# k's transposes in one of the MLP's PSUM banks in two slots, ScalarE's copies a tile later, and k's copies ahead of the division in a third

## The chip, the cores and the metric

The kernel runs on one core of one Trainium2 chip. The time is device microseconds of that core, the median over runs of the whole program. Below, "us" is a microsecond, TensorE is the matrix engine (PE in the profile, its weight loads PEld), VectorE is DVE, ScalarE is ACT, GpSimd is POOL and SyncE is SP.

## The reference

A causal attention with a decay on the scores, and behind it a two-layer MLP over all tokens:

```
q, k, v: (8, 8, 576, 64)   f: (8, 8, 576)   w_in: (512, 2048)   w_out: (2048, 512)
cum    = cumsum(log(clip(f, 1e-4, 1)))
scores = q @ k.T / sqrt(64) + cum[i] - cum[j],  -1e9 above the diagonal
attn   = exp(scores - max) / (sum + 1e-9)
x      = (attn @ v), heads side by side          # (4608, 512)
h      = x @ w_in;  g = h - tanh(h);  out = g @ w_out
```

## The kernel before, in words

**Slots.** The 64 heads are 32 pairs; four pairs make one batch element. The main loop (lines 608 to 629) has a slot p for each pair and one more. `att_items(p)` (line 547) writes out by hand the attention work of a slot, in the order in which every engine gets it, and between these items the loop puts steps of the MLP (`TAKE` says how many). Each engine works its own queue in that order; semaphores are added for what is read and written. So the order on an engine never changes at run time: a late instruction holds up all that stand behind it on its engine.

**A slot's attention.** A pair's scores come in seven tiles, ti = 0 to 6. `scores` (line 306) computes one tile with TensorE into one of two PSUM banks (pool `ps_sc`), and ScalarE takes the exponential of it into SBUF (line 335, tile `e`, or `el` for the small tile 3); from batch element 1 on GpSimd then zeroes what lies above the diagonal (line 345). Tile n + 2 takes the bank of tile n, so its matmuls wait for the exponential of tile n. `values` (line 350) does 30 small matmuls of the pair before, at ti = 2 from slot 5 on, and VectorE divides by the row sums: `rs` (lines 364 and 365) and `xn` (line 366). `turn` (line 369) then transposes `xn` into the MLP's input `XR` with two DMAs of SyncE (lines 380 and 382).

**q's and k's transposes.** For batch elements 0 to 2, `trans` (line 254) brings q and k of a pair into head-dimension-first form (`QT`, `KT`): six TensorE transposes into one PSUM bank (line 264, tile `t`), then two copies out of it, one for the even and one for the odd tokens. They write into the same tile at interleaved places, so the second copy waits for the first. From batch element 3 on DMAs do this, and no PSUM is used.

- Slots 0 to 3: the bank comes from the MLP's pool `ps_m` (three banks).
- Slots 4 to 6: the bank is the single one of the pool `ps_tr`, and VectorE does both copies ("VV", line 277). The transposes of q stand at ti = 0, those of k at ti = 2 in slot 4 and ti = 3 in slots 5 and 6, for the pair of the next slot. In slot 6 the k of slot 7 is made this way.
- Slots 7 and 8 (line 569): each makes two pairs of batch element 2, q at ti = 0, k at ti = 2, q at ti = 4, k at ti = 6, all in the one bank of `ps_tr`. Of each, VectorE does the first copy and ScalarE the second ("VA", lines 277 and 275). Both are emitted right behind the transposes.

**The MLP.** `mlp1` (line 398) is one 128-wide piece of h: four 512-column matmuls into a bank, tanh on ScalarE (line 413), and h - tanh(h) on VectorE (line 417, tile `gq`). For the first 512 tokens the second layer is `mlp2_plain` (line 436): 16 steps of four matmuls (line 442), four steps to an output tile of 128 tokens, which ScalarE copies out of its bank (line 446, tile `ost`) and a DMA of SyncE writes out. Slot 6 holds the last `mlp1` steps of these tokens and the first two steps of `mlp2_plain` fall to slots 6 and 7; slots 7 and 8 hold `mlp2_plain` alone, slot 9 its end and the first `mlp1` of the next 512 tokens. `bank` (line 389) hands out the banks; up to slot 8 these are the three of `ps_m`, from slot 9 on (`widen(1)`, line 613) also that of `ps_tr`.

**Other work there.** In slots 7 and 8 VectorE also forms differences of w_out's blocks (`weights`, line 243, at ti = 1, 3 and 5), GpSimd starts the loads of batch element 3's q and k (line 96), and SyncE transposes that q (line 101).

Of the kernel before, what the change touches and what calls it, by code (L numbers as in the profile page):

```python
# [8 lines left out]
FP32 = mybir.dt.float32  # L9
FP16 = mybir.dt.float16  # L10
AF = mybir.ActivationFunctionType
ALU = mybir.AluOpType
# [9 lines left out]
def kernel(  # L22
# [10 lines left out]
    nc = tc.nc  # L33
    P = 128

    B, H, S, D = q.shape
# [4 lines left out]
    NPAIR = H // 2  # L41
    NJ = 5
# [5 lines left out]
    UW = 512  # L48
# [14 lines left out]
    PSUM = bass.MemoryType.PSUM  # L63
    ps_sc = ctx.enter_context(tc.tile_pool(name="ps_sc", bufs=2, space=PSUM))
    ps_av = ctx.enter_context(tc.tile_pool(name="ps_av", bufs=1, space=PSUM))
    ps_tr = ctx.enter_context(tc.tile_pool(name="ps_tr", bufs=1, space=PSUM))
    ps_m = ctx.enter_context(tc.tile_pool(name="ps_m", bufs=3, space=PSUM))

    win = wpl.tile([P, NCH, DFF], FP16)
    wout = wpl.tile([P, NFT, DM], FP16)  # L70
# [10 lines left out]
    qn, kn = ([t[0:S // NT6, :].rearrange("p (h n d) -> p h n d", h=H, n=NT6) for t in raw] for raw in (qraw, kraw))  # L81
# [170 lines left out]
    E, XN, GQ, SQ, M2 = {}, {}, {}, {}, {}  # L252

    def trans(b, c, src, dst, early, copies, split=False):
        pn, g3 = S // NT6, NT6 // 2
        if early:
            t32 = ps_m.tile([P, UW], FP32, tag="m", name="t32")
            t16 = t32.bitcast(FP16)[:, 0:2 * S // 2].rearrange("p (a g n) -> p a g n", a=2, g=g3)
        else:
            t32 = ps_tr.tile([P, UW], FP32, tag="tr", name="t32")  # L260
            t16 = t32.bitcast(FP16)[:, 0:2 * S // 2].rearrange("p (a g n) -> p a g n", a=2, g=g3)
        for a in range(2):
            for g in range(g3):
                nc.tensor.transpose(out=t16[:, a, g, :],  # L264
                                    in_=src[b % 2][:, 2 * c + a, 2 * g:2 * g + 2, :],
                                    identity=id16[0:pn, 0:pn])
        parts = [(a, e) for a in range(2) for e in range(2)] if split else [(slice(0, 2), e) for e in range(2)]

        def copy(a, e, eng):
            if split:  # L270
                a = slice(a, a + 1)
            to = dst[b % 2][0:D, 2 * c:2 * c + 2, e:S:2].rearrange("d a (p g) -> d a p g", g=g3)[:, a]
            of = t16[e * D:(e + 1) * D, :, :, :].rearrange("d a g p -> d a p g")[:, a]
            if eng == "A":
                nc.scalar.activation(out=to, in_=of, func=AF.Copy)  # L275
            else:
                nc.vector.tensor_copy(out=to, in_=of)  # L277

        todo = [lambda a=a, e=e, eng=eng: copy(a, e, eng) for (a, e), eng in zip(parts, copies)]
        for fn in todo[:2]:  # L280
            fn()
        return todo[2:]

    def head_tiles(a):
        return [[(a, 0, 0, 512, 0)],
                [(a, 1, P, 448, 0), (a, 0, 512, 64, 448)],
                [(a, 2, 2 * P, 320, 0), (a, 3, 3 * P, 192, 320)]]

    TILES = head_tiles(0) + [[(0, 4, 512, 64, 64), (1, 4, 512, 64, 128)]] + head_tiles(1)
    LAST = 3  # L290
# [56 lines left out]

    AV = {}

    def values(b, c, heads=(0, 1)):  # L350
        if 0 in heads:
            AV[(b, c)] = ps_av.tile([P, 2, 512], FP32, tag="av", name="av")
        av = AV[(b, c)][:, :, 0:NJ * (D + 1)].rearrange("p a (i d) -> p a i d", i=NJ)
        for a in heads:
            for ib in range(NJ):
                for j in range(ib + 1):
                    nc.tensor.matmul(out=av[:, a, ib, :], lhsT=E.pop((b, c, a, j, ib)),  # L357
                                     rhs=vn[b % 2][:, j, 2 * c + a, 0:D + 1],
                                     start=(j == 0), stop=(j == ib))
        if 1 not in heads:  # L360
            return
        xn = XN[(b, c)] = fin.tile([P, NJ, P], FP16, tag="xn", name="xn")
        rs = fin.tile([P, 2, NJ, 1], FP32, tag="rs", name="rs")
        nc.vector.tensor_scalar_add(out=rs, in0=av[:, :, :, D:D + 1], scalar1=1e-9)  # L364
        nc.vector.reciprocal(out=rs, in_=rs)
        nc.vector.tensor_tensor(out=xn.rearrange("p i (a d) -> p a i d", a=2), in0=av[:, :, :, 0:D],  # L366
                                in1=rs.to_broadcast([P, 2, NJ, D]), op=ALU.mult)

    def turn(b, c):
        xn = XN.pop((b, c))  # L370
        r0 = b % 4 * S
        if b == 0:
            x32 = ps_m.tile([P, UW], FP32, tag="m", name="x32")
            xt = x32.bitcast(FP16)[:, 0:S]
            for ib in (NJ - 1, 0, 1, 2, 3):
                w0 = min(ib * P, S - P)
                nc.tensor.transpose(out=xt[:, w0:w0 + P], in_=xn[:, ib, :], identity=id16)
            nc.scalar.activation(out=XR[:, c, r0:r0 + S], in_=xt, func=AF.Copy)  # L378
            return
        nc.sync.dma_start_transpose(out=XR[:, c, r0:r0 + S - D].rearrange("p (n t) -> p n t", t=P),  # L380
                                    in_=xn[:, 0:NJ - 1, :].rearrange("p n d -> p (n d)"))
        nc.sync.dma_start_transpose(out=XR[:, c, r0 + S - D:r0 + S], in_=xn[D:P, NJ - 1, :])

    HP = {}
    RINGS = [[ps_m], [ps_m, ps_m, ps_m, ps_tr], [ps_m, ps_m, ps_m, ps_tr, ps_sc, ps_sc]]
    TAGS = {ps_m: "m", ps_tr: "tr", ps_sc: "sc"}
    turn_of = [0, 0]

    def bank(name):
        ring = RINGS[turn_of[0]]  # L390
        pool = ring[turn_of[1] % len(ring)]
        turn_of[1] += 1
        return pool.tile([P, UW], FP32, tag=TAGS[pool], name=name)

    def widen(n):
        turn_of[:] = [n, 0]

    def mlp1(u, ft, part=None):
        if part != 1:
            HP[(u, ft)] = bank("hps")  # L400
        hps = HP[(u, ft)]
        t0 = u * UW % RING
        parts = [(0, t0, min(UW, RING - t0))]
        if t0 + UW > RING:
            parts.append((RING - t0, 0, t0 + UW - RING))
        for o, t, n in parts:
            for ci in {None: range(NCH), 0: range(NCH - 1), 1: (NCH - 1,)}[part]:
                nc.tensor.matmul(out=hps[:, o:o + n], lhsT=win[:, ci, ft * P:(ft + 1) * P],  # L408
                                 rhs=XR[:, ci, t:t + n], start=(ci == 0), stop=(ci == NCH - 1))
        if part == 0:  # L410
            return
        th = tmp.tile([P, UW], FP32, tag="th", name="th")
        nc.scalar.activation(out=th, in_=hps, func=AF.Tanh, scale=-1.0)  # L413
        half, i, kt = ft // NK, ft % NK // 4, ft % 4
        if half == 0 and kt == 0:
            GQ[(u, i)] = gtp.tile([P, 2, NK // 2, UW], FP16, tag="gq", name="gq")
        nc.vector.tensor_tensor(out=GQ[(u, i)][:, half, kt, :], in0=hps, in1=th, op=ALU.add)  # L417
        if u >= PLAIN:
            if ft in (3, 6, 9, 12):
                sums(u, "S3", ft // 3 - 1)  # L420
# [126 lines left out]
    def att_items(p):  # L547
        def put(fn, *args):
            items.append((lambda: fn(*args), True))

        items = []
# [4 lines left out]
        for ti in range(len(TILES)):  # L556
# [9 lines left out]
            for load in LOADS.get((p, ti), ()):  # L566
                items.append((load, False))
            at_q, at_k = (1, 3) if p == 0 else (0, 1) if early else (0, 2) if p == NPAIR else (0, 3)
            if p in (2 * NPAIR - 1, 2 * NPAIR) and ti % 2 == 0:
                pair = pairs[2 * NPAIR + 2 * (p - 2 * NPAIR + 1) + ti // 4]  # L570
                put(trans, *pair, *((kn, KT) if ti % 4 else (qn, QT)), False, "VA")
# [7 lines left out]
            if p == NPAIR:  # L579
                if ti == 1:  # L580
                    put(turn, *pairs[p - 2])
                    put(values, *before)
                    put(mlp1, 0, 0, 0)
                elif ti == 2:
                    put(mlp1, 0, 1, 0)
                    put(turn, *before)
            elif early and ti in (2, 3) and before:
                put(values, *before, (ti - 2,))
            elif not early and ti == 2 and before:
                put(values, *before)  # L590
            if p < NPAIR:
                if ti == 1 and p > 1:
                    put(turn, *pairs[p - 2])
            elif p > NPAIR and ti == 3:
                put(turn, *before)
        return items

# [8 lines left out]
    with tc.manual_schedule(engines=FIVE):  # L606
        bulk()
        for p in range(len(pairs) + 1):
            b, c = divmod(p, NPAIR)
            items = att_items(p)  # L610
            take = TAKE[p] if p < len(TAKE) else 8 - (p - len(TAKE)) % 2
            if p == 2 * NPAIR + 1:
                widen(1)
            mine = mlp[at:at + take]
            at += take
# [5 lines left out]
            given, n = 0, 0  # L621
# [39 lines left out]
```

## Time and profile before

| what | value |
|---|---|
| median of 3 runs | 347.94 us (347.92 to 347.96) |
| the profiled execution's own time | 347.95 us |
| its span from first to last instruction | 346.2 us |
| TensorE busy | 335.2 us, 97% of the span |
| VectorE busy | 261.7 us, 76% |
| ScalarE busy | 232.6 us, 67% |
| GpSimd busy | 161.3 us, 47% |

The profile comes from one execution. A row of its timeline gives the start from the beginning of the span, the busy time, the engine, the line, the operation with its output and input and the count of like instructions merged into the row; in brackets stands how long the engine was idle before, and what released it. TensorE's matmuls are pipelined and the ends in the records are modelled: two rows may overlap, and the step from one start to the next is the safer measure of what a group costs. A chain of waits is followed back from the last instruction, at each step to what released it.

### The profile page before, as it was taken

How to read it: one execution, taken by the hardware profiler on the slowest of the kernel's cores; microseconds unless marked ns; L12 is line 12 of the kernel's file. 1: busy time of each engine (PE TensorE's matmuls, PEld its weight loads, DVE VectorE, ACT ScalarE, POOL GpSimd, SP SyncE). 2: the span in 40 equal slices, each digit the busy share in tenths (PEclk: the TensorE clock that was granted, in tenths of full speed). 3: DMA queues.
4: the chain of work that ended last, by engine and by line, in shares of the span. 5: the costliest groups of instructions: out<-in, count | busy, mean ns of one | idle time of the engine just before them, and what ended most of it. 6: DMA issues, size and time to landing. Idle time of an engine off the chain costs nothing.

```text
span 346.2 us, 8606 instructions
## 1 busy us (share of the span) xinstructions
PE 335.2 (97%) x3253; PEld 230.6 (67%) x3253; DVE 261.7 (76%) x504; ACT 232.6 (67%) x437; POOL 161.3 (47%) x319
## 2 busy tenths in 40 slices
PE   8988998889999999999999999999999999999995
PEld 7476554555578656865688888755875587487485
DVE  6599787564988788678867886788677766876874
ACT  5687886777897787778767876788548842632640
POOL 8974652676558655765577465742322210000000
PEclk9999999999999999999999999999999999999999
DMA  8999999999999999799979997991131013003003
GB/s 108 147 182 201 193 201 154 107 114 177 132 130 105 177 137 122 94 176 137 117 78 200 130 128 78 186 143 27 49 97 31 17 50 110 0 14 109 0 11 113
DMA packets 144877, 38.80 MB, mean 112 GB/s; under 512 B 128148, under 2 KB 143236, under 8 KB 144836
## 3 DMA queue, kind: packets, MB, share of 16 engines
q0 software_dynamic: 92480, 18.39, 69.7%
q1 hardware_dynamic: 52356, 19.88, 30.5%
q8 instruction: 25, 0.41, 0.5%
q14 instruction: 16, 0.13, 0.1%
HBM read 36.85 MB, written 9.44 MB: 134 GB/s over the span
## 4 chain that ended last, share of the span: by engine, by line
PE 87%; DVE 6%; ACT 4%; issue 1%; DMA 1%; ACTq 0%
PE hps L408 32%; PE ops L466 28%; PE ps L326 12%; PE av L357 8%; PE ops L442 3%; DVE gq L417 2%; ACT e L335 2%; DVE QT L277 2%; PE t L264 1%; DVE KT L277 1%; PE ps L329 1%; DMA TQ<-in_f_dram 1%; PE ps L297 1%; ACT QT L275 1%; ACT th L413 1%
## 5 line engine op out<-in xcount | busy, mean ns | idle before, releaser
L408 PE MATMUL hps<-XR,win 128*128 128x512 f16 (+1 forms) x640 | 140.9, 357 | 0.9 <-ACT XR L378 0.7
L413 ACT ACTIVATE th<-hps 128x512 f32<-128x512 f32 x144 | 86.9, 603 | 55.4 <-PE hps L408 54.6
L335 ACT ACTIVATE e<-ps 128x512 f16<-128x512 f32 x192 | 110.5, 598 | 14.1 <-PE ps L326 6.0
L417 DVE TENSOR_TENSOR gq<-hps,th 128x512 f16<-128x512 f32 x144 | 98.4, 688 | 26.0 <-ACT th L413 24.6
L345 POOL TENSOR_SCALAR_AFFINE_SELECT e<-e 128x128 f16<-128x128 f16 x168 | 60.4, 361 | 78.0 <-ACT e L335 76.1
L408 PEld LDWEIGHTS <-win 128*128 128x128 f16 x640 | 57.7, 97 | 48.4 <-issue 0.5
L326 PE MATMUL ps<-QT,KT 67*128 67x64 f16 (+5 forms) x384 | 77.9, 276 | 3.1 <-ACT e L335 1.7
L466 PEld LDWEIGHTS <-gq 128*128 128x128 f16 x640 | 60.4, 97 | 11.1
L466 PE MATMUL ops<-wout,gq 128*128 128x256 f16 x512 | 63.2, 272 | 0.0
L326 PEld LDWEIGHTS <-KT 67*128 67x128 f16 (+1 forms) x384 | 36.7, 98 | 25.5 <-DVE KT L277 1.6
L357 PEld LDWEIGHTS <-e 128*128 128x128 f16 x896 | 32.2, 97 | 3.9
L357 PE MATMUL av<-vn,e 128*128 128x65 f16 x896 | 33.6, 193 | 0.0
L119 POOL DMA_DIRECT2D vn<-in_v_dram x32 | 28.0, 878 | 8.7 <-DMA win<-in_moe_w_in_dram 4.1
L466 PE MATMUL ops<-W,sq 128*128 128x256 f16 x256 | 31.2, 272 | 0.0
L366 DVE TENSOR_TENSOR xn<-av,rs 128x640 f16<-128x640 f32 x32 | 26.4, 825 | 1.1
L466 PEld LDWEIGHTS <-sq 128*128 128x128 f16 x256 | 24.2, 98 | 3.4
L96 POOL DMA_DIRECT2D kn<-in_k_dram x25 | 21.2, 848 | 1.5 <-issue 1.3
L345 POOL TENSOR_SCALAR_AFFINE_SELECT el<-el 128x128 f16<-128x128 f16 x28 | 9.4, 334 | 26.9 <-ACT el L335 26.2
L96 POOL DMA_DIRECT2D qn<-in_q_dram x25 | 21.2, 848 | 1.3 <-issue 0.8
L364 DVE TENSOR_SCALAR rs<-av 128x10 f32<-128x10 f32 x32 | 5.2, 162 | 19.0 <-PE av L357 17.9
L277 DVE COPY QT<-t 64x576 f16<-64x576 f16 x18 | 14.5, 803 | 6.2 <-PE t L264 6.1
L277 DVE COPY KT<-t 64x576 f16<-64x576 f16 (+1 forms) x22 | 16.3, 739 | 3.8 <-PE t L264 3.6
(82 smaller groups left out, 307.5 us busy)
## 6 DMA issues: line engine op xcount, KB each, us to landing
out_dram<-ost SPq DMA_DIRECT2D x34, 256.0 KB
vn<-in_v_dram POOLq DMA_DIRECT2D x24, 128.0 KB, 5.6
qn<-in_q_dram POOLq DMA_DIRECT2D x20, 128.0 KB, 4.3
kn<-in_k_dram POOLq DMA_DIRECT2D x20, 128.0 KB, 4.6
win<-in_moe_w_in_dram POOLq DMA_DIRECT2D x2, 1024.0 KB, 14.8
wout<-in_moe_w_out_dram POOLq DMA_DIRECT2D x2, 1024.0 KB, 14.1
XR<-xn SPq DMA_TRANSPOSE x56
vn<-in_v_dram POOLq DMA_DIRECT2D x12, 64.0 KB, 5.2
```

Source lines behind the costliest of these rows:

```text
L96: nc.gpsimd.dma_start(out=dst[b % 2][0:pn, n, :].rearrange("p (h d) -> p h d", h=H), in_=src[b, :, n * P:n * P + pn, :].rearrange("h p d - ...
L119: nc.gpsimd.dma_start(out=vn[b % 2][:, n, h0:h1, 0:D], in_=v[b, h0:h1, n * P:(n + 1) * P, :].rearrange("h p d -> p h d"))
L277: nc.vector.tensor_copy(out=to, in_=of)
L326: nc.tensor.matmul(out=ps[:, col:col + n], lhsT=KT[b % 2][0:rows, h, j * P:(j + 1) * P], rhs=QT[b % 2][0:rows, h, i0:i0 + n], start=not ow ...
L335: nc.scalar.activation(out=e[:, lo:hi], in_=ps[:, lo:hi], func=AF.Exp, scale=qscale)
L345: nc.gpsimd.affine_select(out=view, in_=view, compare_op=ALU.is_ge, fill=0.0, base=0, pattern=pat, channel_multiplier=-1)
L357: nc.tensor.matmul(out=av[:, a, ib, :], lhsT=E.pop((b, c, a, j, ib)), rhs=vn[b % 2][:, j, 2 * c + a, 0:D + 1], start=(j == 0), stop=(j == ib))
L366: nc.vector.tensor_tensor(out=xn.rearrange("p i (a d) -> p a i d", a=2), in0=av[:, :, :, 0:D], in1=rs.to_broadcast([P, 2, NJ, D]), op=ALU. ...
L408: nc.tensor.matmul(out=hps[:, o:o + n], lhsT=win[:, ci, ft * P:(ft + 1) * P], rhs=XR[:, ci, t:t + n], start=(ci == 0), stop=(ci == NCH - 1))
L413: nc.scalar.activation(out=th, in_=hps, func=AF.Tanh, scale=-1.0)
L417: nc.vector.tensor_tensor(out=GQ[(u, i)][:, half, kt, :], in0=hps, in1=th, op=ALU.add)
L466: nc.tensor.matmul(out=ps[:, m, :], lhsT=LHS[lhs](u, kt // 4)[:, kt % 4, m * P:(m + 1) * P], rhs=rhs[:, kt, :], start=(fresh and (apart or ...
```

## The change

- The three banks of `ps_m` get a tag each (`m0`, `m1`, `m2`), and `m_bank` hands them out in turn, as before. `keep()`, called as slot 7 begins, takes the next one out of the turn until slot 9 begins; there k's transposes go in slots 7 and 8, and the MLP has the other two. q's transposes stay in the bank of `ps_tr`.
- In slots 7 and 8 ScalarE's half of each copy is no longer emitted right behind VectorE's half, but put on a list (`LATER`) that is emptied behind the scores of the next tile (`rest`, at ti = 0, 1, 3 and 5; once more at ti = 0 of slot 9).
- In slot 6 the division of the pair before is put on a list (`HELD`), and so is every addition of `mlp1` that comes while the list is not empty; the list is worked off at ti = 3 behind k's copies. So VectorE's order there becomes k's two copies, `rs`, `xn`, `gq`, `gq` in place of `rs`, `xn`, `gq`, the two copies, `gq`.

The order on TensorE, GpSimd and SyncE stays the same, instruction by instruction, and so does the number and shape of all instructions.

```diff
-    ps_m = ctx.enter_context(tc.tile_pool(name="ps_m", bufs=3, space=PSUM))
+    ps_m = ctx.enter_context(tc.tile_pool(name="ps_m", bufs=1, space=PSUM))
+    M_AT, KEPT = [0], []
+
+    def m_bank(name):
+        while M_AT[0] % 3 in KEPT:
+            M_AT[0] += 1
+        M_AT[0] += 1
+        return ps_m.tile([P, 512], FP32, tag=f"m{(M_AT[0] - 1) % 3}", name=name)
+
+    def keep():
+        while M_AT[0] % 3 in KEPT:
+            M_AT[0] += 1
+        KEPT.append(M_AT[0] % 3)
...
         if early:
-            t32 = ps_m.tile([P, UW], FP32, tag="m", name="t32")
+            t32 = m_bank("t32")
+        elif KEPT and src is kn:
+            t32 = ps_m.tile([P, UW], FP32, tag=f"m{KEPT[0]}", name="t32")
         else:
             t32 = ps_tr.tile([P, UW], FP32, tag="tr", name="t32")
...
-        for fn in todo[:2]:
+        now = 1 if copies == "VA" else 2
+        for fn in todo[:now]:
             fn()
-        return todo[2:]
+        if copies == "VA":
+            LATER.extend(todo[now:])
+        return todo[now:]
...
+    LATER = []
+
+    def rest():
+        while LATER:
+            LATER.pop(0)()
...
+    HELD = []
+
+    def release():
+        while HELD:
+            HELD.pop(0)()
+
-    def values(b, c, heads=(0, 1)):
+    def values(b, c, heads=(0, 1), hold=False):
...
-        nc.vector.tensor_scalar_add(out=rs, in0=av[:, :, :, D:D + 1], scalar1=1e-9)
-        nc.vector.reciprocal(out=rs, in_=rs)
-        nc.vector.tensor_tensor(out=xn.rearrange("p i (a d) -> p a i d", a=2), in0=av[:, :, :, 0:D],
-                                in1=rs.to_broadcast([P, 2, NJ, D]), op=ALU.mult)
+        def divide():
...
+        HELD.append(divide)
+        if not hold:
+            release()
...
-        nc.vector.tensor_tensor(out=GQ[(u, i)][:, half, kt, :], in0=hps, in1=th, op=ALU.add)
+        def add_up():
+            nc.vector.tensor_tensor(out=GQ[(u, i)][:, half, kt, :], in0=hps, in1=th, op=ALU.add)
+        if HELD:
+            HELD.append(add_up)
+        else:
+            add_up()
...
+            if p in (2 * NPAIR - 1, 2 * NPAIR, 2 * NPAIR + 1) and (ti % 2 or ti == 0):
+                items.append((rest, False))
             if p in (2 * NPAIR - 1, 2 * NPAIR) and ti % 2 == 0:
                 pair = pairs[2 * NPAIR + 2 * (p - 2 * NPAIR + 1) + ti // 4]
                 put(trans, *pair, *((kn, KT) if ti % 4 else (qn, QT)), False, "VA")
...
             elif not early and ti == 2 and before:
-                put(values, *before)
+                put(values, *before, (0, 1), p == NPAIR + 2)
...
             elif p > NPAIR and ti == 3:
+                items.append((release, False))
                 put(turn, *before)
...
+            if p == 2 * NPAIR - 1:
+                keep()
             if p == 2 * NPAIR + 1:
+                KEPT.clear()
                 widen(1)
```

More of the change, by code (lines that the diff above doesn't have):

```diff
@@ L256, in trans @@
         if early:
-            t32 = ps_m.tile([P, UW], FP32, tag="m", name="t32")
-            t16 = t32.bitcast(FP16)[:, 0:2 * S // 2].rearrange("p (a g n) -> p a g n", a=2, g=g3)
+            t32 = m_bank("t32")
+        elif KEPT and src is kn:
+            t32 = ps_m.tile([P, UW], FP32, tag=f"m{KEPT[0]}", name="t32")
         else:
             t32 = ps_tr.tile([P, UW], FP32, tag="tr", name="t32")
-            t16 = t32.bitcast(FP16)[:, 0:2 * S // 2].rearrange("p (a g n) -> p a g n", a=2, g=g3)
+        t16 = t32.bitcast(FP16)[:, 0:2 * S // 2].rearrange("p (a g n) -> p a g n", a=2, g=g3)
         for a in range(2):
@@ L363, in values @@
         rs = fin.tile([P, 2, NJ, 1], FP32, tag="rs", name="rs")
-        nc.vector.tensor_scalar_add(out=rs, in0=av[:, :, :, D:D + 1], scalar1=1e-9)
-        nc.vector.reciprocal(out=rs, in_=rs)
-        nc.vector.tensor_tensor(out=xn.rearrange("p i (a d) -> p a i d", a=2), in0=av[:, :, :, 0:D],
-                                in1=rs.to_broadcast([P, 2, NJ, D]), op=ALU.mult)
+        def divide():
+            nc.vector.tensor_scalar_add(out=rs, in0=av[:, :, :, D:D + 1], scalar1=1e-9)
+            nc.vector.reciprocal(out=rs, in_=rs)
+            nc.vector.tensor_tensor(out=xn.rearrange("p i (a d) -> p a i d", a=2), in0=av[:, :, :, 0:D],
+                                    in1=rs.to_broadcast([P, 2, NJ, D]), op=ALU.mult)
+        HELD.append(divide)
+        if not hold:
+            release()
     def turn(b, c):
@@ L372, in turn @@
         if b == 0:
-            x32 = ps_m.tile([P, UW], FP32, tag="m", name="x32")
+            x32 = m_bank("x32")
             xt = x32.bitcast(FP16)[:, 0:S]
@@ L385 @@
     RINGS = [[ps_m], [ps_m, ps_m, ps_m, ps_tr], [ps_m, ps_m, ps_m, ps_tr, ps_sc, ps_sc]]
-    TAGS = {ps_m: "m", ps_tr: "tr", ps_sc: "sc"}
+    TAGS = {ps_tr: "tr", ps_sc: "sc"}
     turn_of = [0, 0]
@@ L392, in bank @@
         turn_of[1] += 1
-        return pool.tile([P, UW], FP32, tag=TAGS[pool], name=name)
+        return m_bank(name) if pool is ps_m else pool.tile([P, UW], FP32, tag=TAGS[pool], name=name)
     def widen(n):
```

## The prediction

> **What bounds the kernel now.** I read the page first, then the busy time by stretches, then the chain of waits in order of time, then TensorE's timeline where that chain leaves TensorE.
>
> ```profile
> span 346.2 us, 8606 instructions
> PE 335.2 (97%) x3253; PEld 230.6 (67%) x3253; DVE 261.7 (76%) x504; ACT 232.6 (67%) x437; POOL 161.3 (47%) x319
> ```
>
> TensorE is the bound as a whole. The stretches (length, then busy time of PE, PEld, DVE, ACT and POOL, granted clock, DMA) tell where it isn't:
>
> ```profile
> 55.32:81.25 25.93, 22.43 (x230) 12.88 (x228) 14.16 (x23) 18.46 (x31) 15.61 (x31) 1.00 1.43 125
> 81.25:283.00 201.75, 201.75 (x2005) 142.69 (x2002) 157.38 (x314) 150.78 (x292) 109.02 (x223) 1.00 1.14 112
> ```
>
> The first stretch runs from the end of slot 6 to the first `mlp1` of slot 9: TensorE's records leave 25.93 - 22.43 = 3.50 us empty. Behind it TensorE has no hole for 201.75 us, so whatever the first stretch gives or loses arrives at the end undiminished, as long as nothing behind it comes late. The chain shows two forms of hole:
>
> ```profile
> 55.00 0.70 DVE KT L277
> 55.71 0.81 DVE KT L277
> ...
> 56.57 0.39 PE ps L326
> ...
> 65.13 0.82 ACT QT L275
> ...
> 66.00 0.43 PE t L264 x6
> ...
> 66.45 0.81 DVE KT L277
> ...
> 67.28 0.82 ACT KT L275
> ...
> 68.14 0.43 PE t L264 x6
> ```
>
> At 56.57 slot 7's first scores wait for k's two copies on VectorE, which stood behind the division. In slots 7 and 8 each set of transposes waits until both copies, one after the other, have emptied the one bank. TensorE's rows give the price of each wait:
>
> ```profile
> 55.09 0.38 PE L326 MATMUL ps<-QT,KT 67*128 67x320 f16 x2
> 56.57 0.39 PE L326 MATMUL ps<-QT,KT 67*128 67x512 f16 x1 [1.10 <-DVE KT L277]
> ...
> 59.00 0.38 PE L326 MATMUL ps<-QT,KT 67*128 67x320 f16 x2
> 59.82 0.41 PE L264 MATMUL t<-id,kn 96*128 96x96 f16 x6 [0.43 <-ACT QT L275]
> ...
> 66.00 0.41 PE L264 MATMUL t<-id,kn 96*128 96x96 f16 x6 [0.42 <-ACT QT L275]
> 66.62 0.38 PE L326 MATMUL ps<-QT,KT 67*128 67x512 f16 x1 [0.21 <-ACT e L335]
> 66.83 1.03 PE L442 MATMUL ops<-wout,gq 128*128 128x512 f16 x4
> 68.14 0.41 PE L264 MATMUL t<-id,qn 96*128 96x96 f16 x6 [0.28 <-ACT KT L275]
> ...
> 73.45 1.03 PE L442 MATMUL ops<-wout,gq 128*128 128x512 f16 x4
> 74.32 0.42 PE L264 MATMUL t<-id,qn 96*128 96x96 f16 x6
> 74.57 0.38 PE L326 MATMUL ps<-QT,KT 67*128 67x448 f16 x2
> ...
> 75.66 0.38 PE L326 MATMUL ps<-QT,KT 67*128 67x320 f16 x2
> 76.47 0.42 PE L264 MATMUL t<-id,kn 96*128 96x96 f16 x6 [0.43 <-ACT QT L275]
> 77.09 0.38 PE L326 MATMUL ps<-QT,KT 67*128 67x512 f16 x1 [0.21 <-ACT e L335]
> ...
> 79.25 0.38 PE L326 MATMUL ps<-QT,KT 67*128 67x320 f16 x2
> 79.48 1.03 PE L442 MATMUL ops<-wout,gq 128*128 128x512 f16 x4
> ```
>
> Ends are modelled, so I measure from start to start. Without a wait a scores tile in two pieces takes 0.23 us (79.25 to 79.48), one in one piece 0.21 (66.62 to 66.83), a step of line 442 0.87 (73.45 to 74.32), six transposes 0.25 (74.32 to 74.57). What a step takes beyond that is wait:
>
> - slot 7's first scores: 56.57 - 55.09 - 0.23 = **1.25**
> - k's transposes behind q's copies, four times, first 59.82 - 59.00 - 0.23 = 0.59, last 76.47 - 75.66 - 0.23 = 0.58: **2.33** in all
> - scores of the next slot's tile 0 behind an exponential that stood behind a copy: 66.62 - 66.00 - 0.25 = 0.37, and the same at 77.09: **0.74**
> - q's transposes behind k's copies: 68.14 - 66.83 - 0.87 = **0.44**
>
> Sum 4.76 us. The records' 3.50 is the lower bound, since the modelled ends cover part of each wait.
>
> **The change part by part.** It adds and removes no instruction, and the order on TensorE, GpSimd and SyncE is the old one. It moves copies on ScalarE and the division on VectorE, and takes waits away. These rows carry the steps:
>
> ```profile
> 53.13 0.16 DVE L364 TENSOR_SCALAR rs<-av 128x10 f32<-128x10 f32 x1
> ...
> 54.92 1.60 DVE L277 COPY KT<-t 64x576 f16<-64x576 f16 x2
> 54.45 1.71 ACT L335 ACTIVATE e<-ps 128x512 f16<-128x512 f32 x3
> 65.97 1.09 ACT L335 ACTIVATE e<-ps 128x512 f16<-128x512 f32 x2
> ...
> 80.54 0.60 ACT L446 ACTIVATE ost<-ops 128x512 f32<-128x512 f32 x1 [0.21 <-PE ops L442]
> 74.78 0.80 DVE L277 COPY QT<-t 64x576 f16<-64x576 f16 x1 [0.37 <-PE t L264]
> L417 DVE TENSOR_TENSOR gq<-hps,th 128x512 f16<-128x512 f32 x144 | 98.4, 688 | 26.0 <-ACT th L413 24.6
> 39.54 0.78 POOL L90 DMA_DIRECT2D kn<-in_k_dram  x1
> kn<-in_k_dram POOLq DMA_DIRECT2D x1, 576.0 KB, 17.1
> 75.12 1.23 SPq L382 DMA_TRANSPOSE XR<-xn  x1
> 286.31 1.22 SPq L382 DMA_TRANSPOSE XR<-xn  x1
> 290.53 4.70 PE L408 MATMUL hps<-XR,win 128*128 128x512 f16 x21
> ```
>
> *Slot 6, the division behind the copies.* The copies take the place of `rs` at 53.13 and end 1.60 later, at 54.73 instead of 56.52. The wait doesn't vanish: next in line is the bank. Tile 0 takes the bank of slot 6's tile 5, whose exponential is the second of the three from 54.45. Two exponentials take 1.09 and one 0.60, so one starts 0.49 after the other: 54.94 to 55.54, and with the 0.05 from 56.52 to 56.57 the scores start at 55.59. Gain 0.98, left over 55.59 - 55.09 - 0.23 = 0.27. The division, over by 54.92 before, ends by 54.92 + 1.60 = 56.5; the work in sum is the same, so the two `gq` still end by 56.52 + 0.69 = 57.2, the first of them by 56.6. Nobody waits for these: the last `gq` is read by the layer-two step behind k's transposes, which moves to 58.5 (below), and slot 7's `values`, which need the division's input bank, come one step later, near 59.4.
>
> *Slots 7 and 8, k in a bank of its own.* k's transposes no longer wait for q's copies, nor q's for k's. Each now waits for the copies of the set before in the same bank, three or four tiles earlier. Tight is only k at slot 8's tile 2, behind k's set of slot 7's tile 6. ScalarE's copy there stands behind `ost`. From the start of the layer-two step before, `ost` starts 1.06 later (79.48 to 80.54), the copy 0.49 after it (a pass of 0.60 like the exponential), ends 0.82 later, and TensorE follows 0.04 behind: 2.41. TensorE itself needs 0.87 + 0.25 + 0.23 + 0.87 + 0.23 = 2.45. In time by 0.04; I price it 0 to 0.2.
>
> *ScalarE's copies a tile later.* No scores wait for these copies soon, but the exponentials behind them are waited for two tiles on. The tightest is slot 8's tile 6, behind q's copy, needed by slot 9's tile 1. From q's transposes VectorE's copy starts 0.45 later (66.00 to 66.45, the same for k; VectorE was idle 0.37 ahead of it at 74.78), ScalarE's 0.83 after that (66.45 to 67.28), the exponential 0.84 after that (65.13 to 65.97), ends 0.60 later: 2.72, and 0.04 until TensorE starts, 2.76. TensorE needs 0.25 + 0.23 + 0.87 + 0.23 + 0.25 + 0.21 + 0.87 = 2.91. In time by 0.15. In slot 7 another set of transposes stands between, so the margin is 0.25 more. The 0.74 go.
>
> *What comes late next.* All loads issued before slot 6 keep their hour while TensorE arrives earlier: k of batch element 2 lands at 39.54 + 17.1 = 56.6, and its first transposes move from 59.82 to 59.82 - 0.98 - 0.59 = 58.25, the step behind them to 58.5. The first `mlp1` of slot 9 reads what SyncE's transposes bring: the last ends its issue at 76.35, 4.90 ahead of 81.25. The waits taken out between them (0.58 and 0.37) leave 3.95. Nearest row: at the end of the kernel 290.53 - 287.53 = 3.0 were enough without a wait.
>
> *Sum.* 4.76 - 0.27 = 4.49 taken out; I allow about 0.05 for the 0.04 margin. The profiled execution took 347.95 (span 346.2 and 1.75 around it), the median of the runs is 347.94, so both bases agree. 347.95 - 4.45 = **343.5 us**.
>
> **The rivals.**
>
> *A: ScalarE gives part back.* The margins of 0.04 and 0.15 are small. If ScalarE is late at all eight copies by what an exponential behind a copy cost here (0.37), 3.0 return: 346.5. For: ScalarE is busy 18.46 us of a stretch that shrinks to 25.93 - 4.45 = 21.5, 86%. Against: it has still 3 us free, and the two margins are the worst of the eight places.
>
> *B: two banks are too few for layer two.* Each output tile's first step would wait until `ost` of the one before has emptied its bank. At 80.54 `ost` starts 0.20 behind the next group's start (80.34 = 79.48 + 0.86) and ends 0.60 later, so a group right behind it would wait 0.8. Two groups in slots 7 and 8 begin with only transposes and a scores tile between (0.48): 0.3 each, up to 0.84 more where a copy stands in front of `ost`. Taken as 0.8 each: 343.5 + 1.6 = 345.1. Against: two groups alternate, and one is 3.5 us of matmuls, so the bank of the last but one is long empty. The Trainium skill speaks for B: its page "Perfetto Trace Analysis" (Optimizing Tensor Performance, Matmuls) has independent groups rotate through different PSUM banks, so that emptying one overlaps the next. By that rule k's transposes gain what the MLP loses; the trace agrees with the first half (0.58 a time in the shared bank), and no row of this run shows the second.
>
> *C: the waits stay.* The copies still follow each other, and if k's new bank were held as long by the MLP as the old one was by q, nothing would move: 347.9. Against: its last user is a `gq` that ends by 56.6 at the latest, 1.6 ahead of k.
>
> *D, slower: ScalarE stands still in front of VectorE's copies.* Its copy must wait for VectorE's, with exponentials behind it. At the four sets of q VectorE's copy could come late, since the division or a `weights` step stands in front. A late one costs a copy and the exponential's turn, 0.84 + 0.81, less the margin of 0.15: 1.5 a set, 6.0 for the four, 349.5. It decides the sign from about 1.1 a set (4.45 / 4). Against: VectorE was idle 0.37 ahead of such a copy, and has 14.16 us of work in the stretch.
>
> **How the numbers follow.** Forecast (343.0 to 344.3) 0.72; A 0.11; B 0.05; C 0.04; D 0.08. The low end is all 4.76 and a little more gone (343.0, with 0.2 for reading), the high end reaches over the forecast's unknowns, B and the cheaper third of A: 345.4. Two runs of this kernel can be told apart from about 0.2%, 0.7 us. Faster by more: forecast, A and B, 0.88. Within: C, 0.04. Slower: D, 0.08.
>
> **What would show it.** In the changed profile TensorE's rows should hold no wait for QT's or KT's copies in slots 7 and 8, one of about 0.3 for an exponential at slot 7's first scores (near 55.6), and the first `mlp1` of slot 9 near 76.8 instead of 81.25, with the rest shifted as a whole. Waits of scores for exponentials would speak for A, of line 442 for `ost` for B, ScalarE idle in front of copies with TensorE waiting behind for D. I am wrong if the first `mlp1` of slot 9 moves forward and the end doesn't.

## The result and the profile after

The changed kernel takes 344.37 us (344.34 to 344.58), the kernel before 347.94 (347.92 to 347.96): a ratio of 0.9898, 95% interval 0.9886 to 0.9910. Faster by 3.57 us where 4.45 were forecast. The profiled execution took 344.34 against 347.95.

The page of the changed kernel, first its head, then the shares of the chain that ended last:

```profile
span 342.6 us, 8607 instructions
PE 334.8 (98%) x3253; PEld 231.2 (67%) x3253; DVE 261.8 (76%) x504; ACT 233.1 (68%) x437; POOL 162.3 (47%) x319
...
PE 96%; ACT 2%; DVE 0%; issue 0%; ACTq 0%
```

The five counts are as before (the one more of 8607 is in none of them), and the busy times differ by 1.0 us at most (GpSimd); the span is 3.6 us shorter. In the chain VectorE's share has gone from 6% to nothing.

Busy time by stretches of the changed kernel, in the same columns as before; the first begins 0.25 us ahead of slot 7's first scores and ends at slot 9's first `mlp1`:

```profile
56.00:77.61 21.61, 21.46 (x229) 12.73 (x227) 14.21 (x23) 18.64 (x31) 16.66 (x31) 1.00 1.68 138
77.61:283.00 205.39, 205.39 (x2052) 145.99 (x2049) 160.11 (x321) 151.22 (x292) 108.98 (x223) 1.00 1.08 113
```

TensorE's records leave 0.15 us of the stretch empty, where 3.50 were, and behind it there is again no hole. So the gain arrived at the end whole, as the prediction had it. ScalarE now works 18.64 of 21.61 us, and TensorE waits for it in two places only, 0.25 and 0.19 us (both below).

TensorE's timeline of the changed kernel, at the places whose waits the prediction priced:

```profile
58.67 0.38 PE L348 MATMUL ps<-QT,KT 67*128 67x320 f16 x2
58.90 0.42 PE L277 MATMUL t<-id,kn 96*128 96x96 f16 x6
59.15 1.03 PE L483 MATMUL ops<-wout,gq 128*128 128x512 f16 x4
...
64.50 0.42 PE L277 MATMUL t<-id,kn 96*128 96x96 f16 x6
64.75 0.38 PE L348 MATMUL ps<-QT,KT 67*128 67x512 f16 x1
64.97 1.03 PE L483 MATMUL ops<-wout,gq 128*128 128x512 f16 x4
65.83 0.42 PE L277 MATMUL t<-id,qn 96*128 96x96 f16 x6
...
67.18 0.38 PE L348 MATMUL ps<-QT,KT 67*128 67x320 f16 x2
67.60 0.42 PE L277 MATMUL t<-id,kn 96*128 96x96 f16 x6
...
77.61 1.03 PE L442 MATMUL hps<-XR,win 128*128 128x512 f16 x4
```

k's transposes follow the scores 0.23 later (58.67 to 58.90), which is no wait. The scores behind them follow after 0.25 (64.50 to 64.75) and q's transposes 0.86 behind the layer-two step. One wait is left here: 67.60 - 67.18 - 0.23 = 0.19, k's transposes at slot 8's tile 2.

The chain of the changed kernel, in order of time, at slot 7's first scores:

```profile
54.59 0.45 PE ps L348 x3
55.12 1.09 ACT e L357 x2
56.25 0.38 PE ps L348
```

The scores start at 56.25, released by an exponential and no longer by VectorE. Their predecessor starts at 55.77 (the three rows merged below), so the wait is 56.25 - 55.77 - 0.23 = 0.25.

Here is what doesn't fit. That predecessor started at 55.09 before: the changed kernel arrives 0.68 us **late** at the place where its gains begin. From there to slot 9's first `mlp1` it takes 77.61 - 55.77 = 21.84 us in place of 81.25 - 55.09 = 26.16, so 4.32 are gained, and 4.32 - 0.68 = 3.64 remain. The loss stands in slot 4, in the rows of the changed kernel's TensorE:

```profile
35.56 0.38 PE L348 MATMUL ps<-QT,KT 67*128 67x448 f16 x2
36.70 1.02 PE L442 MATMUL hps<-XR,win 128*128 128x512 f16 x4 [0.75 <-DVE gq L453]
...
55.77 0.86 PE L348 MATMUL ps<-QT,KT 67*128 67x320 f16 x3
```

and in the same rows of the kernel before:

```profile
35.58 0.38 PE L326 MATMUL ps<-QT,KT 67*128 67x448 f16 x2
35.80 1.03 PE L408 MATMUL hps<-XR,win 128*128 128x512 f16 x4
...
47.52 1.02 PE L408 MATMUL hps<-XR,win 128*128 128x512 f16 x4 [0.20 <-DVE gq L417]
```

An `mlp1` step of slot 4, which started without a wait, now waits 0.92 us (36.70 - 35.56 - 0.22) for VectorE's `gq`. About 0.2 of it comes back at 47.52, where the kernel before waited for a `gq` and the changed one, being later, doesn't.

### The profile page after: what moved, and what is told of

Same layout as the page of the kernel before. It is cut to its first block, busy times and chain, and to the rows that moved or that the text cites. A ratio compares the mean times of both kernels' runs of the same rounds, so it can differ in the third digit from the quotient of the medians.

```text
span 342.6 us, 8607 instructions
## 1 busy us (share of the span) xinstructions
PE 334.8 (98%) x3253; PEld 231.2 (67%) x3253; DVE 261.8 (76%) x504; ACT 233.1 (68%) x437; POOL 162.3 (47%) x319
## 4 chain that ended last, share of the span: by engine, by line
PE 96%; ACT 2%; DVE 0%; issue 0%; ACTq 0%
PE hps L442 36%; PE ops L507 29%; PE ps L348 13%; PE av L385 8%; PE ops L483 4%; PE idle L556 2%; PE t L277 2%; ACT e L357 1%; PE ps L351 1%; PE ps L319 1%; PE ps L317 0%; PE x L411 0%; ACT th L447 0%; DVE gq L453 0%; ACT XR L412 0%
## 5 line engine op out<-in xcount | busy, mean ns | idle before, releaser
L367 POOL TENSOR_SCALAR_AFFINE_SELECT e<-e 128x128 f16<-128x128 f16 x168 | 61.3, 366 | 72.3 <-ACT e L357 70.0
```

Source lines behind the costliest of these rows:

```text
L367: nc.gpsimd.affine_select(out=view, in_=view, compare_op=ALU.is_ge, fill=0.0, base=0, pattern=pat, channel_multiplier=-1)
```

## The experiments

**Theory 1.** The mechanism of the prediction holds in slots 6 to 9. What is missing was lost by the hand-out of the MLP's banks, which the change rewrote for the whole kernel. The kernel before had one pool of three, and by this theory a new tile got the bank that had come free first. In slot 4 two `mlp1` tiles are open over a `turn` of batch element 0 whose tile ScalarE empties early; the next `mlp1` then got that tile's bank. With three tags in a strict turn it gets the bank of the older `mlp1`, which tanh and `gq` still read. **Theory 2.** That is harmless, and the shortfall came from ScalarE's margins (rival A) or from two banks being too few for the MLP (rival B).

Eight kernels were run. Line numbers in their rows are those of their own files. The kernel before, run beside each group of them, had a median of 347.94 to 347.96 us. The diffs of e3 to e8 are against e2, that of e2 is against the changed kernel, that of e1 against the kernel before.

**e1_turn: the strict turn alone**, on the kernel before.

```diff
-    ps_m = ctx.enter_context(tc.tile_pool(name="ps_m", bufs=3, space=PSUM))
+    ps_m = ctx.enter_context(tc.tile_pool(name="ps_m", bufs=1, space=PSUM))
+    M_AT, KEPT = [0], []
+    def m_bank(name):
...
```

> The kernel before with one thing of the change: the MLP's three banks are handed out in a strict turn; no bank kept for k, ScalarE's copies and the division where they were. Theory 1 (the 0.87 us that the changed kernel lacks against 343.5 were lost in slot 4, where the strict turn gives an mlp1 step the bank of the mlp1 two before, still being read, in place of the one that ScalarE had already emptied): TensorE waits 0.90 there, 0.2 of it comes back at a later wait for the same thing, so 347.94 + 0.68 = 348.6 us. Theory 2 (the turn is harmless, and the shortfall arose in slots 7 and 8 from ScalarE's margins or from the MLP's two banks): 347.9 us.

Measured 348.64 us, ratio 1.0020 (1.0012 to 1.0029): slower by 0.70. TensorE's rows of this kernel hold the wait:

```profile
35.59 0.38 PE L346 MATMUL ps<-QT,KT 67*128 67x448 f16 x2
36.72 1.02 PE L440 MATMUL hps<-XR,win 128*128 128x512 f16 x4 [0.75 <-DVE gq L451]
```

**e2_turn_mended: the changed kernel with the old hand-out in slot 4.**

```diff
             x32 = m_bank("x32")
+            if c == NPAIR - 1:
+                M_AT[0] -= 1
```

> The changed kernel, where only the second transposed pair of slot 4 gives its bank on to the mlp1 step behind it, as in the kernel before. Theory 1: the wait of 0.90 in slot 4 is gone, the one of 0.2 is back, 344.37 - 0.68 = 343.7 us, and the first mlp1 of slot 9 starts near 76.9. Theory 2: 344.4 us.

Measured 343.65 us, ratio 0.9877 (0.9863 to 0.9890), 0.72 below the changed kernel. Its rows in slots 4, 8 and 9:

```profile
35.58 0.38 PE L348 MATMUL ps<-QT,KT 67*128 67x448 f16 x2
35.80 1.03 PE L444 MATMUL hps<-XR,win 128*128 128x512 f16 x4
...
66.50 0.38 PE L348 MATMUL ps<-QT,KT 67*128 67x320 f16 x2
66.93 0.41 PE L277 MATMUL t<-id,kn 96*128 96x96 f16 x6
...
76.94 1.03 PE L444 MATMUL hps<-XR,win 128*128 128x512 f16 x4
```

The wait in slot 4 is gone, slot 9's first `mlp1` starts at 76.94, and the wait of 0.20 in slot 8 (66.93 - 66.50 - 0.23) stays. With e1 that decides for theory 1: 0.7 us one way and the other. That the old pool goes by what comes free first is concluded from this; no view shows which bank a tile got. The next kernels build on e2.

**e3_ost_behind: ScalarE's copy of k ahead of the output copy** in slot 8's tile 0.

```diff
-            if here and (p > 0 or ti > 1):
+            if p == 2 * NPAIR and ti == 0:
+                put(lambda: (scores(*here, 0), rest()))
+            elif here and (p > 0 or ti > 1):
                 put(scores, *here, ti)
```

> The mended kernel of e2, and in slot 8 ScalarE's copy of k stands right behind the exponential of tile 0, ahead of the output copy of the second layer. Theory 1 (k's transposes at slot 8's tile 2 waited 0.19 for that copy, which stood behind the output copy): the 0.19 go, 343.7 - 0.2 = 343.5 us, the predicted time. Rival: the exponential behind comes late by the same amount or the wait falls to another, 343.7 us.

Measured 343.45 us, ratio 0.9871 (0.9858 to 0.9884). The last wait of slot 8 is gone in its rows:

```profile
66.51 0.38 PE L348 MATMUL ps<-QT,KT 67*128 67x320 f16 x2
66.73 0.42 PE L277 MATMUL t<-id,kn 96*128 96x96 f16 x6
```

The 0.20 between e2 and e3 is less than the 0.7 us from which the prediction held two runs to be apart, but the runs of either kernel agree within 0.04 us. This is the fastest of all the kernels here, 0.92 below the changed one.

**e4_no_hold: the division of slot 6 back ahead of k's copies.**

```diff
-                put(values, *before, (0, 1), p == NPAIR + 2)
+                put(values, *before)
```

> The mended kernel of e2 with the division of slot 6 back ahead of k's copies. If that part is worth what the prediction said, slot 7's first scores wait 1.25 again in place of 0.27: 343.7 + 0.98 = 344.7 us. If later margins absorb it (the copies or exponentials of slot 7 being what TensorE meets next): under 344.2 us.

Measured 344.64 us, 0.99 above e2. TensorE's rows show the old wait, 56.53 - 55.08 - 0.23 = 1.22:

```profile
55.08 0.38 PE L348 MATMUL ps<-QT,KT 67*128 67x320 f16 x2
56.53 0.39 PE L348 MATMUL ps<-QT,KT 67*128 67x512 f16 x1 [1.08 <-DVE KT L290]
```

**e8_division_only: the division moved, and nothing else.**

```diff
-        now = 1 if copies == "VA" else 2
+        now = 2
...
-        elif KEPT and src is kn:
-            t32 = ps_m.tile([P, UW], FP32, tag=f"m{KEPT[0]}", name="t32")
...
-            if p == 2 * NPAIR - 1:
-                keep()
```

> The kernel before with the division of slot 6 behind k's copies and nothing else of the change (banks as before, copies right behind each other, one bank for q and k). If this part stands by itself, slot 7's first scores come 0.98 earlier and all else shifts: 347.94 - 0.98 = 346.96 us, and with e2, e5 and e6 the four cases of bank and late copies are complete: none 346.96, bank alone 345.36, late copies alone 347.76, both 343.65. If what it gains is lost again at q's and k's transposes, which wait for copies and not for TensorE: above 347.4 us.

Measured 347.01 us, ratio 0.9978 (0.9968 to 0.9989). The kernel before took 347.96 beside it, so this part is worth nearly the same alone (0.95) as on top of the others (0.99): a shift of TensorE as a whole, with nothing given back. The other waits are as they were, in the view of waits of this kernel from 54 to 81 us (us in total, times, longest):

```profile
PE t L275 <- ACT QT L286: 1.7, 4, 0.4
PE ps L346 <- ACT e L355: 0.4, 2, 0.2
PE t L275 <- ACT KT L286: 0.3, 1, 0.3
```

**e5_copies_not_late: k keeps its bank, ScalarE's copies stand right behind VectorE's.**

```diff
-        now = 1 if copies == "VA" else 2
+        now = 2
```

> The mended kernel of e2, with ScalarE's copies right behind VectorE's again; k keeps its bank. By the same hand count as in the prediction: k's transposes no longer wait, but the scores two groups behind them need an exponential that now stands behind q's copy: from q's transposes VectorE's copy 0.45, ScalarE's copy 0.83 later, exponential 0.84 later, 0.60 long: 2.76, against 1.83 for TensorE, a wait of 0.93 at tile 0 of slots 8 and 9; without the 0.19 of slot 8's tile 2: 343.7 + 1.86 - 0.19 = 345.4 us. Rival (the bank alone does it, the copies' place is a detail): 343.7 us or less.

Measured 345.36 us. TensorE's rows of this kernel:

```profile
63.80 0.42 PE L277 MATMUL t<-id,kn 96*128 96x96 f16 x6
65.02 0.38 PE L348 MATMUL ps<-QT,KT 67*128 67x512 f16 x1 [0.79 <-ACT e L357]
...
73.25 0.42 PE L277 MATMUL t<-id,kn 96*128 96x96 f16 x6
74.47 0.38 PE L348 MATMUL ps<-QT,KT 67*128 67x512 f16 x1 [0.80 <-ACT e L357]
```

k's transposes don't wait any more, but the scores behind them do, 65.02 - 63.80 - 0.25 = 0.97 each time. Before, these two places cost 0.58 + 0.37 = 0.95. At tile 6 the bank alone saves nothing: the wait moves from the transposes to the exponential that stands behind q's copy.

**e6_no_bank: copies a tile later, but q and k share the one bank.**

```diff
-        elif KEPT and src is kn:
-            t32 = ps_m.tile([P, UW], FP32, tag=f"m{KEPT[0]}", name="t32")
...
-            if p == 2 * NPAIR - 1:
-                keep()
```

> The mended kernel of e2, but k's transposes share the one bank with q's again; copies a tile later and the division as in the change. k's transposes wait for q's copies behind one more exponential, 0.57 each, four times; the two waits of scores (0.37 each) are gone; q's transposes at slot 8's tile 0 wait for k's copy behind an exponential and the output copy, about 1.5. Left over 2.3 + 1.5 against 0.19: 343.7 + 3.6 = 347.3 us. Rival (the late copies do it, not the bank): below 345.5 us.

Measured 347.76 us against 347.95 for the kernel before (interval of the ratio 0.9993 to 1.0021): not to be told from it, and 0.75 above e8, from which it differs by the late copies. TensorE's rows:

```profile
64.23 0.38 PE L346 MATMUL ps<-QT,KT 67*128 67x320 f16 x2
65.11 0.41 PE L275 MATMUL t<-id,kn 96*128 96x96 f16 x6 [0.50 <-ACT QT L286]
65.36 0.38 PE L346 MATMUL ps<-QT,KT 67*128 67x512 f16 x1
65.58 1.03 PE L483 MATMUL ops<-wout,gq 128*128 128x512 f16 x4
68.12 0.42 PE L275 MATMUL t<-id,qn 96*128 96x96 f16 x6 [1.51 <-ACT KT L286]
```

k's transposes wait 65.11 - 64.23 - 0.23 = 0.65 (four places alike, so 2.6), and q's 68.12 - 65.58 - 0.87 = 1.67. I had expected 0.57 and 1.5, so the time came out 0.46 above the count; the places and their order were right. Late copies without a second bank put an exponential and the output copy into the loop that empties the bank.

Together with e8 and e2 this gives the four cases, all with the division moved and the old hand-out in slot 4:

| us | copies right behind | copies a tile later |
|---|---|---|
| q and k in one bank | 347.01 (e8) | 347.76 (e6) |
| k in a bank of its own | 345.36 (e5) | 343.65 (e2) |

The bank alone gains 1.65, the late copies alone lose 0.75, both gain 3.36. Apart they would add up to 0.90, so 2.46 of the 3.36 exist only in the pair: they are one change.

**e7_one_mlp_bank: a second bank of the MLP's lies unused** in slots 7 and 8.

```diff
                 keep()
+                keep()
```

> The mended kernel of e2, but a second of the MLP's banks lies unused through slots 7 and 8, so each output tile of the second layer needs the one bank that the tile before has just left. By the prediction's rival B, made real: the second output tile of slot 8's waits about 0.45 for the output copy ahead of it, the next 0.37, the one in slot 7 behind the values 0.05, the first mlp1 of slot 9 about 0.1: 343.7 + 0.9 = 344.6 us; by B's own price of 0.8 each 345.3 us. If the two banks of the change had already been too few, e2 would show waits of line 442's matmuls for the output copy, and the loss here would be smaller.

Measured 344.27 us, 0.62 above e2. TensorE's rows:

```profile
65.41 0.39 PE L348 MATMUL ps<-QT,KT 67*128 67x448 f16 x2
66.08 1.02 PE L485 MATMUL ops<-wout,gq 128*128 128x512 f16 x4 [0.28 <-ACT ost L489]
66.94 0.38 PE L348 MATMUL ps<-QT,KT 67*128 67x320 f16 x2
67.17 0.42 PE L277 MATMUL t<-id,kn 96*128 96x96 f16 x6
...
71.45 0.39 PE L348 MATMUL ps<-QT,KT 67*128 67x448 f16 x2
72.05 1.02 PE L485 MATMUL ops<-wout,gq 128*128 128x512 f16 x4 [0.21 <-ACT ost L489]
```

The two larger waits came as counted (0.44 and 0.37); the two small ones (0.05 and about 0.1) did not. The wait of 0.44 comes just ahead of k's transposes at slot 8's tile 2 and covers their 0.20 (66.94 to 67.17 is no wait), so 0.61 is left and the time came out 0.33 below the count. This is what too few banks look like and cost; the changed kernel has none of these rows, so two banks are enough there.

## Why the prediction was right, and by how much it missed

The forecast time of 343.5 missed by 0.87 us. The sign was right, and so was the cause of the gain. The whole range (343.0 to 345.4) held, but in part by luck: 344.37 lies just above the forecast's own part of it (343.0 to 344.3), in the room left for the rivals A and B, and what filled it was for the most part a loss that the prediction did not have.

- **The price of the waits, 4.76 us from start to start.** Right: 4.32 were gained in the stretch, and 0.25 + 0.19 are left over, which adds up to 4.76. The lower bound from the records (3.50) was too low, since a waiting group's modelled end covers part of its wait.
- **Slot 6, gain 0.98, left over 0.27.** Measured 0.99 (e4) and 0.95 (e8); left over 0.25, and for the reason given, the exponential of slot 6's tile 5.
- **Slots 7 and 8, k's own bank.** The waits went. At the one tight place the step that failed is "the copy 0.49 after it", behind the output copy. In the changed kernel ScalarE's rows read:

```profile
65.13 1.08 ACT L357 ACTIVATE e<-ps 128x512 f16<-128x512 f32 x2
66.11 0.60 ACT L487 ACTIVATE ost<-ops 128x512 f32<-128x512 f32 x1
66.73 0.81 ACT L288 ACTIVATE KT<-t 64x576 f16<-64x576 f16 x1
67.57 0.60 ACT L357 ACTIVATE e<-ps 128x512 f16<-128x512 f32 x1
```

  From the output copy to the copy of k it is 0.62, not 0.49, and the output copy itself started 0.08 later than counted (66.11 - 64.97 = 1.14 after the layer-two step, not 1.06), held by the exponential. So the margin of 0.04 became a wait of 0.19. The 0 to 0.2 that the prediction allowed for it held; the 0.05 that went into the sum did not. I had taken the step between two exponentials for that between any two instructions of ScalarE.
- **Copies a tile later, the 0.74.** Right, and e5 shows that without this part they would have grown to 1.94 (two times 0.97). It was closer than counted: the exponential that slot 9's tile 1 needs started at 73.84 and took 0.60, and TensorE, which starts 0.04 behind it, came at 74.53, so of the margin of 0.15 only 0.05 was left.
- **What comes late next.** The last of SyncE's transposes ended its issue 3.96 us ahead of slot 9's first `mlp1`; predicted 3.95, without a wait. k of batch element 2 was there in time: its first transposes, at 58.90, did not wait.
- **The order on TensorE stays, waits are only taken away.** This is what failed. The order did stay, but the change rewrote how banks are handed out in all slots, and the description of the change took "in turn, as before" for what the pool did. The sum has no term for this. It cost 0.68 in slot 4, outside the stretch that the prediction looked at, and makes up nearly all of the miss: 343.5 + 0.68 + 0.14 (the wait in slot 8, priced at 0.05) = 344.3.
- **The rivals.** A came at one of its eight places only, the copy of k above, with 0.19 and not 3.0. But for the 0.25 at slot 7's first scores, which the sum has, no scores waited for an exponential in slots 7 to 9. B did not come; e7 shows its form. Its price of 1.6 was too high: 0.81 for the two waits, 0.62 in the end. The rule of the Trainium skill's page "Perfetto Trace Analysis" (Optimizing Tensor Performance, Matmuls), that independent groups of matmuls rotate through different PSUM banks, bears on both halves of the change. The traces agree with it: with one bank for q's and k's transposes the waits stand in e8, with one bank for the MLP in e7. For the MLP two banks were enough. C is refuted by e2 against e8 (3.36 gained). D did not come: TensorE waited for no copy of q in slots 7 and 8.

## What to carry to other kernels

A second buffer helps only if the engine that empties it doesn't stand in the way elsewhere: here the copies had to move behind an exponential that TensorE needs sooner. The bank alone gained less than half of what both gain, and the late copies alone lost. Price such a pair as a loop, from the start of a producer back to its next start, with each engine's queue in it.

A change in how buffers are handed out reaches every user of the pool, and not only the stretch that it is meant for. Look for the waits that the whole program gains, first of all those of the engine that sets the end.

## What the runs showed of the hardware

In the changed kernel ScalarE starts an exponential 0.48 us after the one before, though each takes 0.60 in its record (the two from 65.13 take 1.08). Behind the output copy, which takes 0.60 too, the copy of k (64 partitions, 576 columns) starts only after 0.62 (66.11 to 66.73), and behind that copy, which takes 0.81, the next exponential starts after 0.84 (66.73 to 67.57). Neither of these waited for data: VectorE's half of k's copy had ended at 65.75, and the scores that the exponential reads had been started at 66.09. So in these rows the step between two instructions of ScalarE depends on the pair. Why, no run here tells.
